# Linear attention on one core: the normaliser's sum over a head's partitions made by accumulating DMA transfers instead of a TensorE product

## The chip, the cores and the metric

The kernel runs on one core of a Trainium2 chip. The metric is the device time of one execution in microseconds; lower is better. Times of a kernel are medians of several runs. A profile is one execution recorded by the hardware profiler; its span runs from the first to the last recorded instruction.

## The reference

Linear attention with 32 heads of 20 dimensions on 2048 rows of 640 columns, in bfloat16:

```python
B, S, D = x.shape                       # 1, 2048, 640
H = 32; Dh = D // H                     # 20
q, k, v = (x @ wqkv) split into heads
phi = lambda t: where(t > 0, t + 1, exp(t)) + 1e-6
pq, pk = phi(q), phi(k)
kv  = einsum("bhsd,bhse->bhde", pk, v)
z   = pk summed over the rows           # one vector of 20 per head
num = einsum("bhqd,bhde->bhqe", pq, kv)
den = einsum("bhqd,bhd->bhq", pq, z) + 1e-6
out = (num / den, heads joined) @ wo
```

The change concerns `den`: for each row and head, the sum over the head's 20 dimensions of pq times z.

## The kernel before

The work is written out by hand as a list of operations for each engine, in program order. A small planner (`Plan.add`, L35) notes what each operation reads and writes and puts in the semaphore waits; each engine then runs its own list strictly in order (`emit`, L76). TensorE (PE) multiplies, ScalarE (ACT) takes exponentials and logarithms and empties PSUM banks, VectorE (DVE) does the rest of the elementwise work, SyncE (SP) issues nearly all transfers, and GpSimd (POOL) makes constants at the start (`pool_const`, L145).

Stages, in the order of TensorE's list:

1. k = x wk for 16 tiles of 128 rows (L292), phi on ScalarE and VectorE (L305, L307, L310).
2. P = xᵀ phi(k) in two halves of 320 columns (`p_step`, L319). The first half runs over all 16 row tiles, then the second. Five PSUM banks (0 to 4) hold the sums; `p_out` (L331, L334) copies them out. VectorE adds phi(k) over the rows meanwhile (`z_steps`, L366, L387).
3. The queries, in 20 tiles (`q_tile`, L345) of 128 columns by 512 rows: five matmuls each, then an exponential (L353) on ScalarE and two VectorE operations (L357, L360). They are strewn into the second stage and go on behind it. Block s (0 to 3) means rows 512 s to 512 s + 511; each block has five tiles c. The columns are permuted so that partition p of a tile belongs to head p // 4: a head has four partitions in each of the five tiles, 20 in all.
4. `kv_group` (L423) makes kv from P and wv, `kv_mask` (L440) keeps the diagonal blocks, `w2_group` (L447, L451) multiplies by wo, and `w2_rows` (L459) carries the six pieces of the product to their rows with SP transfers.
5. The output: 16 tiles of 128 rows, pq times w2 (`out_mm`, L487), evacuated on ScalarE and VectorE (L524, L509, L512) and sent out by SP (L497).

The normaliser runs beside this. `z_finish` (L397, L401) turns the sums over rows into a column vector zc, with five small matmuls and a VectorE copy. `wsum` (L408, L412) adds pq times zc over the five tiles of a block: one ScalarE operation and four on VectorE, the last into `ub` in bfloat16. `den` (L465) is one TensorE product of `ub` with the head mask `hm`, which sums the four partitions of each head and gives all four the sum. `den_act` (L470, L472) takes the logarithm and exp(-x) of it on ScalarE, into `rd`. `normalize` (L479) multiplies the five pq tiles of the block by `rd` on VectorE, in place; the output products read them.

What sets the order is the main part at the end of the function. `next_q(n)` puts in one query tile and then takes n operations from the list `todo`; `work` appends weighted sums ("w") or normalisations ("n") to it, `pop` takes some off. `inverse(s)` puts in `den` and `den_act` of block s. PSUM banks for query tiles, z and `den` come from a rotating list (`take`): banks 5, 6, 7, and bank 4 as well once the second half of P has been copied out.

Of the kernel before, what the change touches and what calls it, by code (L numbers as in the profile page):

```python
# [82 lines left out]
def bass_standalone__linear_attn_block__prompt_kernel(nc, x, wqkv, wo, out):  # L83
# [11 lines left out]
    with contextlib.ExitStack() as ctx:  # L95
        es = ctx.enter_context

        def sb(name, cols, dt=BF16):
            return es(nc.sbuf_tensor(name, [128, cols], dt))
# [25 lines left out]
        ident = sb("ident", 128)  # L125
        lb = [sb(f"lb{j}", BK, F32) for j in range(2)]
        rd = [sb(f"rd{j}", 2 * BK) for j in range(2)]
        DUO = range(9)
        osb = [sb(f"osb{j}", D) for j in range(4)]
        ps = es(nc.psum_tensor("ps", [128, 8 * BK], F32))  # L130
# [3 lines left out]
        def bank(b, n=BK, off=0, parts=128):  # L134
            return ps[0:parts, BK * b + off:BK * b + off + n]
# [80 lines left out]
        def xT_keys(a, b, cs=range(NC_)):  # L216
            keys = []
            for i, (p, q) in enumerate(XCH):
                if p < b and a < q:
                    keys += [("xT", i)] if i >= NPE else sorted(  # L220
                        {("xT", i, 0 if c < 2 else 2) for c in cs})
            return keys
# [113 lines left out]

        nq = [0]

        def q_tile(sbk, c, b, between=None):
            i = nq[0] % 3  # L340
            nq[0] += 1

            def mm(e):
                for d in range(NC_):
                    r = e.matmul(  # L345
                        bank(b), wqp[:, d * D + 128 * c:d * D + 128 * c + 128],
                        xT[:, d * S + BK * sbk:d * S + BK * (sbk + 1)],
                        start=(d == 0), stop=(d == NC_ - 1))
                return r
            P.add("pe", mm, reads=[("wqp", d) for d in range(NC_)]  # L350
                  + xT_keys(BK * sbk, BK * (sbk + 1)), writes=[("bank", b)])
            t = eq[i]
            P.add("act", lambda e: e.activation(t[:, :], bank(b), ACTF.Exp),  # L353
                  reads=[("bank", b), "table"], writes=[("eq", i)])
            if between:
                between()
            P.add("dve", lambda e: e.tensor_scalar(  # L357
                t[:, :], t[:, :], 1.0, 1e-6, ALU.min, ALU.add),
                reads=[("eq", i)], writes=[("eq", i)])
            P.add("dve", lambda e: e.scalar_tensor_tensor(  # L360
                pq[:, c * S + BK * sbk:c * S + BK * (sbk + 1)], bank(b), 0.0, t[:, :],
                ALU.max, ALU.add),
                reads=[("bank", b), ("eq", i)], writes=[("pq", sbk, c)])
# [40 lines left out]
        def wsum(s, c):  # L404
            v = pq[:, c * S + BK * s:c * S + BK * (s + 1)]
            a, z, key = ua[s % 2], zc[:, c:c + 1], ("ua", s % 2)
            if c == 0:
                P.add("act", lambda e: e.activation(a[:, :], v, ACTF.Copy, scale=z),  # L408
                      reads=[("pq", s, c), "zc"], writes=[key])
                return  # L410
            dst, dkey = (ub[s % 2], ("ub", s % 2)) if c == NC_ - 1 else (a, key)
            P.add("dve", lambda e: e.scalar_tensor_tensor(  # L412
                dst[:, :], v, z, a[:, :], ALU.mult, ALU.add),
                reads=[("pq", s, c), "zc", key], writes=[dkey])
# [49 lines left out]
        def den(s, b):  # L464
            P.add("pe", lambda e: e.matmul(bank(b), hm[:, :], ub[s % 2][:, :], start=True, stop=True),  # L465
                  reads=["hm", ("ub", s % 2)], writes=[("bank", b)])

        def den_act(s, b):
            t = lb[s % 2]
            P.add("act", lambda e: e.activation(t[:, :], bank(b), ACTF.Ln, bias=eps[:, 0:1]),  # L470
                  reads=[("bank", b), "eps", "table"], writes=[("lb", s % 2)])
            P.add("act", lambda e: e.activation(  # L472
                rd[s // 2][:, BK * (s % 2):BK * (s % 2 + 1)], t[:, :], ACTF.Exp, scale=-1.0),
                reads=[("lb", s % 2)], writes=[("rd", s)])
# [94 lines left out]
        def take():  # L569
            small.append(small.pop(0))  # L570
            return small[-1]

        def next_q(n=1, between=None):
            q_tile(*qs.pop(0), take(), between)
            for _ in range(n):
                if todo:
                    todo.pop(0)()
# [13 lines left out]
        def pop(n):  # L591
            for _ in range(n):
                todo.pop(0)()
# [12 lines left out]
        p_out(0)  # L606
        next_q()
        next_q()
        for st in range(NT - 2):
            p_step(1, st)  # L610
            if st in (0, 1):
                zst.pop(0)()
            if st == 5:
                z_finish(take())
                work("w0", "w1", "n0")
                pop(3)
            if st in (1, 4, 7, 10, 12):
                next_q({7: 2, 10: 2}.get(st, 0))
            if st == 11:
                inverse(0)  # L620
        assert not zst
        for d in range(NC_):
            p_step(1, NT - 2, (d,))
            p_step(1, NT - 1, (d,))
        p_out(1)
        pop(3)

        def state_groups():
            kv_group(0)
            kv_mask(0)  # L630
        next_q(0, between=state_groups)
        small.insert(0, 4)

        def first_groups():
            w2_group(0, 2)
# [9 lines left out]
        w2_group(5, 0)  # L645
        next_q(1)
        next_q(1)
        inverse(1)
        work("w20", "n1", "w21234")
        for n in (1, 2, 2):  # L650
            next_q(n)
# [51 lines left out]
```

## Time and profile before

| | |
|---|---|
| median of 3 runs | 99.36 us (99.22 to 99.4) |
| the profiled execution | 99.4 us |
| its span | 98.1 us |
| granted TensorE clock | 1.0 |
| instructions | 1667 |
| transfers | 11.73 MB, all on queues of SP and ACT |
| GpSimd's busy time | 3.5 us, all at the start |

A row of a timeline gives the start and the length in microseconds, the engine, the line of the kernel, the operation, its output and inputs, how many instructions were merged, and in brackets how long the engine had been idle before and what it waited for. "PEld" is TensorE's loading of weights, which runs beside the matmuls. Consecutive matmuls overlap, so a row's length is somewhat longer than the time that it adds to the stream; the chain of work that ended last gives the added time.

### The profile page before, as it was taken

What the parts mean: (1) busy time and instruction counts of PE and PEld (TensorE: products, weight loads), DVE (VectorE), ACT (ScalarE), POOL (GpSimd) and SP (SyncE); (2) the same over time, 40 slices, a digit from 0 to 9 for tenths busy, and PEclk for the clock granted to TensorE, in tenths of its full rate; (3) what the DMA queues carried; (4) which work ended last, traced back from release to release, by engine and by line L of the source; (5) the groups of instructions that cost most, each with busy time, mean ns of one, the idle gap of its engine ahead of it and who ended that gap; (6) DMA issues with size and microseconds to landing.
All of it is one profiled execution on the core that took longest, in us unless ns stands there. A gap on an engine that the chain in (4) does not pass through costs nothing.

```text
span 98.1 us, 1667 instructions
## 1 busy us (share of the span) xinstructions
PE 95.0 (97%) x651; PEld 62.4 (64%) x657; DVE 74.0 (75%) x138; ACT 50.3 (51%) x83; POOL 3.5 (4%) x15
## 2 busy tenths in 40 slices
PE   6999999999999999999999999999999999999991
PEld 2667777777777666555566556755447776677771
DVE  0305987888889897999849759999979998819332
ACT  5107454445698201462042476289796749665321
POOL 6800000000000000000000000000000000000000
DMA  2986899989999920000000000006600223322534
GB/s 47 361 193 131 162 169 135 218 272 379 366 362 284 205 63 10 0 0 0 0 7 0 0 0 0 0 0 165 164 15 0 98 102 134 134 70 73 197 134 134
DMA packets 17236, 11.73 MB, mean 120 GB/s; under 512 B 9933, under 2 KB 17229, under 8 KB 17229
## 3 DMA queue, kind: packets, MB, share of 16 engines
q1 hardware_dynamic: 16653, 11.10, 42.9%
q10 hardware_dynamic: 576, 0.53, 1.6%
q8 instruction: 5, 0.08, 0.4%
q14 instruction: 2, 0.02, 0.1%
HBM read 5.90 MB, written 2.62 MB: 87 GB/s over the span
## 4 chain that ended last, share of the span: by engine, by line
PE 90%; DVE 6%; ACT 1%; issue 0%
PE ps L292 23%; PE ps L487 22%; PE ps L345 21%; PE ps L319 17%; DVE za L366 3%; PE ps L280 3%; PE ps L447 2%; PE ps L423 1%; DVE pq L360 1%; ACT eq L353 1%; PE ps L198 1%; PE ps L465 1%; DVE eq L357 1%; DVE pt L334 0%; DVE osb L512 0%
## 5 line engine op out<-in xcount | busy, mean ns | idle before, releaser
L319 PE MATMUL ps<-pk,xn 128*128 128x320 bf16 x160 | 24.0, 299 | 0.0
L345 PE MATMUL ps<-xT,wqp 128*128 128x512 bf16 x95 | 23.1, 379 | 0.3
L292 PE MATMUL ps<-wk,xT 128*128 128x320 bf16 x160 | 22.9, 305 | 0.0
L487 PE MATMUL ps<-w2p,pq 128*128 128x320 bf16 (+3 forms) x170 | 22.3, 291 | 0.1
L353 ACT ACTIVATE eq<-ps 128x512 bf16<-128x512 f32 x20 | 11.9, 597 | 19.2 <-PE ps L345 19.0
L319 PEld LDWEIGHTS ps<-pk,xn 128*128 128x128 bf16 x160 | 15.6, 98 | 7.5
L292 PEld LDWEIGHTS ps<-wk,xT 128*128 128x128 bf16 x160 | 15.9, 100 | 6.5 <-ACT xT L210 0.2
L487 PEld LDWEIGHTS ps<-w2p,pq 128*128 128x128 bf16 x170 | 15.9, 98 | 6.4 <-DVE pq L479 0.2
L305 ACT ACTIVATE ek<-ps 128x640 bf16<-128x640 f32 x16 | 11.2, 704 | 11.8 <-PE ps L292 11.1
L345 PEld LDWEIGHTS ps<-xT,wqp 128*128 128x128 bf16 x100 | 9.7, 97 | 9.2
L360 DVE SCALAR_TENSOR_TENSOR pq<-ps,eq 128x512 bf16<-128x512 f32 x20 | 13.8, 692 | 0.7
L310 DVE SCALAR_TENSOR_TENSOR pk<-ps,ek 128x640 bf16<-128x640 f32 x16 | 13.2, 825 | 0.5
L412 DVE SCALAR_TENSOR_TENSOR ua<-pq,zc,ua 128x512 f32<-128x512 bf16 x12 | 9.0, 749 | 1.1 <-ACT ua L408 0.9
L307 DVE TENSOR_SCALAR ek<-ek 128x640 bf16<-128x640 bf16 x16 | 5.2, 324 | 5.9 <-ACT ek L305 5.9
L479 DVE TENSOR_TENSOR pq<-pq,rd 128x512 bf16<-128x512 bf16 x20 | 7.4, 418 | 2.8 <-ACT rd L472 2.8
L357 DVE TENSOR_SCALAR eq<-eq 128x512 bf16<-128x512 bf16 x20 | 5.8, 289 | 4.1 <-ACT eq L353 3.9
L524 ACT CAST osb<-ps 128x640 bf16<-128x640 f32 x9 | 6.2, 688 | 3.6 <-PE ps L487 3.4
L512 DVE CAST osb<-ps 128x320 bf16<-128x320 f32 (+2 forms) x8 | 3.5, 434 | 3.3 <-PE ps L487 3.1
L366 DVE TENSOR_TENSOR za<-pk 128x1280 f32<-128x1280 bf16 x4 | 5.8, 1483 | 0.0
L509 ACT CAST osb<-ps 128x320 bf16<-128x320 f32 (+1 forms) x8 | 3.1, 404 | 4.7 <-PE ps L487 4.5
L366 DVE TENSOR_TENSOR za<-za 128x1280 f32<-128x1280 f32 x3 | 4.4, 1482 | 0.0
L270 ACT COPY wqp<-wqn 128x640 bf16<-128x640 bf16 x5 | 4.3, 933 | 0.0
(41 smaller groups left out, 43.5 us busy)
## 6 DMA issues: line engine op xcount, KB each, us to landing
out_dram<-osb SPq DMA_DIRECT2D x15, 160.0 KB, 1.8
xn<-in_x_dram SPq DMA_DIRECT2D x2, 800.0 KB, 10.1
wqn<-in_wqkv_dram SPq DMA_DIRECT2D x1, 800.0 KB, 6.4
wv<-in_wqkv_dram SPq DMA_DIRECT2D x1, 800.0 KB, 13.6
wog<-in_wo_dram SPq DMA_DIRECT2D x1, 750.0 KB, 14.2
w2p<-w2g SPq DMA_DIRECT2D x5, 150.0 KB
xn<-in_x_dram SPq DMA_DIRECT2D x1, 640.0 KB, 7.6
wk<-in_wqkv_dram SPq DMA_DIRECT2D x3, 160.0 KB, 3.4
```

Source lines behind the costliest of these rows:

```text
L292: r = e.matmul(bank(b + h, HALF), xT[:, c * S + 128 * st:c * S + 128 * st + 128], wk[:, c * D + HALF * h:c * D + HALF * (h + 1)], start=(c ...
L305: P.add("act", lambda e: e.activation(fold(t[:, :]), two_banks(b), ACTF.Exp), reads=banks + ["table"], writes=[("ek", st % 3)])
L310: P.add("dve", lambda e: e.scalar_tensor_tensor(fold(pk[:, st * D:(st + 1) * D]), two_banks(b), 0.0, fold(t[:, :]), ALU.max, ALU.add), rea ...
L319: r = e.matmul(bank(d, HALF), xn[:, st * D + 128 * d:st * D + 128 * d + 128], pk[:, st * D + HALF * h:st * D + HALF * (h + 1)], start=(st ...
L345: r = e.matmul(bank(b), wqp[:, d * D + 128 * c:d * D + 128 * c + 128], xT[:, d * S + BK * sbk:d * S + BK * (sbk + 1)], start=(d == 0), sto ...
L353: P.add("act", lambda e: e.activation(t[:, :], bank(b), ACTF.Exp), reads=[("bank", b), "table"], writes=[("eq", i)])
L357: P.add("dve", lambda e: e.tensor_scalar(t[:, :], t[:, :], 1.0, 1e-6, ALU.min, ALU.add), reads=[("eq", i)], writes=[("eq", i)])
L360: P.add("dve", lambda e: e.scalar_tensor_tensor(pq[:, c * S + BK * sbk:c * S + BK * (sbk + 1)], bank(b), 0.0, t[:, :], ALU.max, ALU.add), ...
L366: P.add("dve", lambda e: e.tensor_tensor(d_ap, a, b, ALU.add), reads=ra + rb, writes=[dst])
L412: P.add("dve", lambda e: e.scalar_tensor_tensor(dst[:, :], v, z, a[:, :], ALU.mult, ALU.add), reads=[("pq", s, c), "zc", key], writes=[dkey])
L479: P.add("dve", lambda e: e.tensor_tensor(v, v, rd[i][:, BK * o:BK * (o + 1)], ALU.mult), reads=[("rd", sbk), ("pq", sbk, c)], writes=[("pq ...
L487: r = e.matmul(bank(b, hi - lo), pq[:, c * S + 128 * st:c * S + 128 * st + 128], w2p[:, c * D + lo:c * D + hi], start=(c == 0), stop=(c == ...
```

## The change

For blocks 0 and 1 (rows 0 to 1023) the last weighted sum goes into a new float32 tile `uf`, and the sum over a head's four partitions is made by five transfers in SBUF. Part k is the partitions k, k + 4, k + 8 and so on of `uf`, each delivered to the four partitions of its head. SP copies part 0 into `sa` and part 2 into `sc`. GpSimd then issues three accumulating transfers: part 1 is added to `sa`, part 3 to `sc`, and at last `sc` to `sa`. `den_act` reads `sa`. Blocks 2 and 3 are as before.

In the order: z's products and its copy stand directly behind the matmuls of the seventh query tile, ahead of that tile's exponential, and all five weighted sums of block 0 follow there; they stood one row tile of P later and were strewn between the next tiles. The block's logarithm and exponential move from before the tenth query tile's exponential to behind that of the eleventh; those of block 1 stay behind the seventeenth. The sums of block 1 keep their place but for one operation.

```diff
+        uf = [sb(f"uf{j}", BK, F32) for j in range(2)]
+        sa = [sb(f"sa{j}", BK, F32) for j in range(2)]
+        sc = [sb(f"sc{j}", BK, F32) for j in range(2)]
...
-        def q_tile(sbk, c, b, between=None):
+        def q_tile(sbk, c, b, between=None, behind=None):
...
+            if behind:
+                behind()
             t = eq[i]
             P.add("act", lambda e: e.activation(t[:, :], bank(b), ACTF.Exp),
...
-            dst, dkey = (ub[s % 2], ("ub", s % 2)) if c == NC_ - 1 else (a, key)
+            dst, dkey = (a, key) if c < NC_ - 1 else (
+                (uf[s], ("uf", s)) if s < 2 else (ub[s % 2], ("ub", s % 2)))
...
+        def head_sum(s):
+            def part(k):
+                return uf[s][k:128:4, :].unsqueeze(1).broadcast_to([32, 4, BK])
+
+            def move(eng, dst, src, reads, key, **kw):
+                P.add(eng, lambda e: e.dma_start(dst[:, :], src, **kw),
+                      reads=reads + ([key] if kw else []), writes=[key], dma=True)
+            a, c = ("sa", s), ("sc", s)
+            move("sp", sa[s], part(0), [("uf", s)], a)
+            move("sp", sc[s], part(2), [("uf", s)], c)
+            move("pool", sa[s], part(1), [("uf", s)], a, accum_op=ALU.add)
+            move("pool", sc[s], part(3), [("uf", s)], c, accum_op=ALU.add)
+            move("pool", sa[s], sc[s][:, :], [c], a, accum_op=ALU.add)
+
         def den_act(s, b):
             t = lb[s % 2]
-            P.add("act", lambda e: e.activation(t[:, :], bank(b), ACTF.Ln, bias=eps[:, 0:1]),
-                  reads=[("bank", b), "eps", "table"], writes=[("lb", s % 2)])
+            src, key = (sa[s][:, :], ("sa", s)) if b is None else (bank(b), ("bank", b))
+            P.add("act", lambda e: e.activation(t[:, :], src, ACTF.Ln, bias=eps[:, 0:1]),
+                  reads=[key, "eps", "table"], writes=[("lb", s % 2)])
...
+        def first_sum():
+            z_finish(take())
+            work("w0")
+            pop(5)
+            head_sum(0)
+            work("w1")
+
         for st in range(NT - 2):
             p_step(1, st)
             if st in (0, 1):
                 zst.pop(0)()
-            if st == 5:
-                z_finish(take())
-                work("w0", "w1", "n0")
-                pop(3)
-            if st in (1, 4, 7, 10, 12):
-                next_q({7: 2, 10: 2}.get(st, 0))
-            if st == 11:
-                inverse(0)
+            if st in (1, 7, 10, 12):
+                next_q({7: 3, 10: 1}.get(st, 0))
+            if st == 4:
+                next_q(0, behind=first_sum)
...
         p_out(1)
-        pop(3)
+        pop(1)
+        head_sum(1)
...
         next_q(0, between=state_groups)
         small.insert(0, 4)
+        den_act(0, None)
+        work("n0")
...
-        inverse(1)
+        den_act(1, None)
```

More of the change, by code (lines that the diff above doesn't have):

```diff
@@ L571, in take, with next_q @@
             return small[-1]
-        def next_q(n=1, between=None):
-            q_tile(*qs.pop(0), take(), between)
+        def next_q(n=1, between=None, behind=None):
+            q_tile(*qs.pop(0), take(), between, behind)
             for _ in range(n):
```

## The prediction, made before the changed kernel ran

> **What bounds the kernel now.** I read the page first: busy shares, slices, the chain that ended last. Then, for the stretch that the change touches, the merged timeline of all engines from 47 to 74 us, the weight loads, and the waits of SP's queue. The page:
>
> ```profile
> PE 95.0 (97%) x651; PEld 62.4 (64%) x657; DVE 74.0 (75%) x138; ACT 50.3 (51%) x83; POOL 3.5 (4%) x15
> PE   6999999999999999999999999999999999999991
> PE 90%; DVE 6%; ACT 1%; issue 0%
> ```
>
> TensorE is busy in every slice but the ends; between its first and last matmul it hardly waits. So the time is the sum of TensorE's matmuls: a matmul taken away is time gained, and any wait put before a matmul is time lost, at one to one, for nothing behind it has slack to give back. GpSimd works 3.5 us in all. The chain that ended last, in order of time, shows what the two removed products weigh, and a query tile's five matmuls:
>
> ```profile
> 47.73 1.08 PE ps L345 x5
> ...
> 55.85 0.22 PE ps L465
> ...
> 70.50 0.22 PE ps L465
> ```
>
> L465 is the product with the head mask, one for each 512 rows. Each adds 0.22 us to TensorE's stream; for rows 0 to 1023 there are two. **Gain: 2 x 0.22 = 0.44 us**, and no more, whatever the rest does.
>
> **The change part by part.** Times are in the clock of the profiled execution, span 98.1 us, time 99.40 us; the 1.30 us around the span I leave as they are. The median of the runs is 99.36, so the execution lies 0.04 above it.
>
> The rows that I walk along, from the timeline of all engines:
>
> ```profile
> 46.38 1.32 DVE L387 TENSOR_TENSOR zs<-za 128x640 bf16<-128x640 f32 x1
> 47.57 1.24 PE L345 MATMUL ps<-xT,wqp 128*128 128x512 bf16 x5
> 47.93 0.69 DVE L360 SCALAR_TENSOR_TENSOR pq<-ps,eq 128x512 bf16<-128x512 f32 x1
> 49.33 0.27 PE L397 MATMUL ps<-ones,zs 128*128 128x1 bf16 x5
> 49.81 0.69 DVE L360 SCALAR_TENSOR_TENSOR pq<-ps,eq 128x512 bf16<-128x512 f32 x1
> 50.41 0.15 DVE L401 COPY zc<-ps 128x5 f32<-128x5 f32 x1
> 50.60 0.72 ACT L408 ACTIVATE ua<-pq,zc 128x512 f32<-128x512 bf16 x1 [1.16 <-DVE zc L401]
> 51.45 1.54 DVE L412 SCALAR_TENSOR_TENSOR ua<-pq,zc,ua 128x512 f32<-128x512 bf16 x2 [0.88 <-ACT ua L408]
> 52.91 0.29 DVE L357 TENSOR_SCALAR eq<-eq 128x512 bf16<-128x512 bf16 x1
> 53.23 0.69 DVE L360 SCALAR_TENSOR_TENSOR pq<-ps,eq 128x512 bf16<-128x512 f32 x1
> 53.93 1.24 PE L345 MATMUL ps<-xT,wqp 128*128 128x512 bf16 x5
> ```
>
> *z moved up.* The five z products now come right behind the seventh query tile, whose stream ends at 48.65 (1.08 from 47.57), before the next five state matmuls and not behind them. Their operand zs is complete at 46.38 + 1.32 = 47.70, so they don't wait, and they only change places on TensorE: cost 0. Their result is there at 48.65 + 0.27 = 48.92; VectorE, free since 47.93 + 0.69 = 48.62, copies it at 48.95 and not at 50.41.
>
> *Weighted sums moved up.* ScalarE's first scaling began 0.19 behind the copy (50.41 to 50.60) and VectorE's first addition 0.85 behind that (51.45). So in the new order ScalarE starts at 49.14 and VectorE at 50.0. All four additions now run in one go, ahead of the seventh tile's own two operations. Four such additions stand later in the same trace:
>
> ```profile
> 77.52 2.32 DVE L412 SCALAR_TENSOR_TENSOR ua<-pq,zc,ua 128x512 f32<-128x512 bf16 x3
> 79.87 0.75 DVE L412 SCALAR_TENSOR_TENSOR ub<-pq,zc,ua 128x512 bf16<-128x512 bf16 x1
> 80.54 2.32 DVE L412 SCALAR_TENSOR_TENSOR ua<-pq,zc,ua 128x512 f32<-128x512 bf16 x3
> ```
>
> From 77.52 to 80.54 are 3.02 us for four. The fourth starts 2.35 behind the first and takes 0.75: uf of rows 0 to 511 is written at 50.0 + 3.10 = **53.10** (ub was finished at 54.61 + 0.75 = 55.36 before). A bf16 or float32 result makes no difference (0.75 and 0.77 each). The seventh tile's pair follows at 53.02 and ends 0.33 + 0.69 later, at **54.04**, where it ended at 49.81 + 0.69 = 50.50.
>
> *What this delay holds up.* The query tiles go round three PSUM banks and z takes a turn: tile 7 has bank 5, z 6, tile 8 bank 7, tile 9 bank 5 again. Tile 9's first matmul runs at 53.93 and its weights are loaded ahead:
>
> ```profile
> 53.79 0.88 PEld L345 LDWEIGHTS ps<-xT,wqp 128*128 128x128 bf16 x5
> 64.73 0.60 PEld L447 LDWEIGHTS ps<-wog,kvt 120*120 120x120 bf16 x4
> ```
>
> Now it must wait for tile 7's pair, 54.04 and an assumed 0.03 for the signal. If only the matmul waits, TensorE stands 0.14 us; if the weight load waits too, which starts 0.14 ahead of its matmul, 0.28. Below the two ends lies nothing, for VectorE can't be through earlier than its rows allow. I take the middle: **0.21 us lost**. So from tile 9 on, TensorE has lost 0.21 and saved 0.22, and the old clock holds again. Tiles 10 and 11 have banks 6 and 7, free since 49.1 and about 55. VectorE goes on from 53.96, with 0.33 + 0.60 for a pair until the next operation begins (49.81 to 50.41) and 0.75 for an addition: tile 8's pair until 54.9, two additions of the second block until 56.4, tile 9's pair until 57.3, the third addition until 58.1. Tile 10's pair began at 58.49 when its exponential was there (row below), and does so again, after 0.4 of idle time. The state copies L334 stand where they were.
>
> *Rows 512 to 1023.* Their last addition follows the state copies (below), at 60.22, so uf is written at 60.97. VectorE then has 1.5 us less in front of the mask products, which TensorE didn't wait for visibly: 0.
>
> *The sum over DMA.* In place of one product and its wait, five transfers in three levels, each with its semaphore: SP copies parts 0 and 2 into sa and sc (256 KB each; each of 32 partitions goes to four), GpSimd adds part 1 to sa and part 3 to sc, then adds sc to sa. The trace has no GpSimd transfer and no accumulating one. The nearest rows are SP's:
>
> ```profile
> out_dram<-osb SPq DMA_DIRECT2D x15, 160.0 KB, 1.8
> ```
> ```profile
> L497 SPq DMA_DIRECT2D out_dram<-osb x16: 332/332/382, 76.1 to 96.2; - x16
> DMA to landing us min/median/max: 1.6/1.8/3.7
> ```
> ```profile
> L459 SPq DMA_DIRECT2D w2p<-w2g x6: 697/772/932, 64.7 to 69.3; - x6
> ```
>
> A landing is 1.6 to 3.7 us, 1.8 in the middle, for 160 KB. For SP's copies of 256 KB I put 2.0, an estimate a little above that. An accumulating one reads two operands and is built by another engine; I take 2.8, midway between 1.8 and 3.7. Then: 2.0 for sa, 0.35 until sc has landed (one SP issue of 0.33), 2.8 and 2.8 for the two GpSimd levels, 0.3 assumed for three signals: **T = 8.3 us** from uf to the end, estimated. The lowest the rows allow is 3 x 1.6 + 0.35 = 5.2, the highest 3 x 3.7 + 0.35 + 0.3 = 11.8, or 13.3 with an issue of 0.77 before each GpSimd level.
>
> *Who waits for it.* ScalarE's logarithm, now behind the exponential of tile 11 (at 60.98). What is queued behind it on ScalarE: the exponential of tile 12, the copies of the w2 groups, and through these TensorE.
>
> ```profile
> 56.31 0.68 ACT L470 ACTIVATE lb<-ps,eps 128x512 f32<-128x512 f32 x1
> 57.02 0.63 ACT L472 ACTIVATE rd<-lb 128x512 bf16<-128x512 f32 x1
> 58.49 0.29 DVE L357 TENSOR_SCALAR eq<-eq 128x512 bf16<-128x512 bf16 x1 [0.97 <-ACT eq L353]
> 59.43 0.88 DVE L334 CAST pt<-ps 128x320 bf16<-128x320 f32 x2
> 60.22 1.53 DVE L412 SCALAR_TENSOR_TENSOR ua<-pq,zc,ua 128x512 f32<-128x512 bf16 x2
> 60.78 1.59 PE L423 MATMUL ps<-pt,wv 128*128 128x120 bf16 x30
> 60.98 0.60 ACT L353 ACTIVATE eq<-ps 128x512 bf16<-128x512 f32 x1 [0.65 <-PE ps L345]
> 63.50 0.60 ACT L353 ACTIVATE eq<-ps 128x512 bf16<-128x512 f32 x1 [1.92 <-PE ps L345]
> 63.99 0.69 ACT L451 CAST w2g<-ps 120x640 bf16<-120x640 f32 x1
> 71.03 0.68 ACT L470 ACTIVATE lb<-ps,eps 128x512 f32<-128x512 f32 x1
> 73.79 0.43 PE L487 MATMUL ps<-w2p,pq 128*128 128x320 bf16 x2
> ```
>
> ScalarE is idle for 1.92 us between 61.58 and 63.50. Logarithm and exponential take 0.71 + 0.63 = 1.34 together (0.04 more if an SBUF operand costs what L408's 0.72 shows): they fit there at no cost if the sum has landed by 63.50 - 1.34 = **62.16**. Beyond that the copy of w2 group 0 (63.99 to 64.68) comes late, and its banks are wanted by the load at 64.73: no slack left. From 53.10 this gives the chain **9.06 us**. With T = 8.3 it lands at 61.4, 0.76 early: cost 0. If that cover is gone, each us of lateness costs one.
>
> *The second sum* starts at 60.97 and is wanted at 71.03, where the logarithm stood before: 10.06 us, so 0 too; and TensorE needs rows 512 to 1023 only four output tiles behind 73.79. Its GpSimd transfers wait behind the first sum's last issue (about 58.5), long past. On SP its two issues stand before the first w2 transfer; SP waits there anyway:
>
> ```profile
> SPq L459 <- ACT w2g L451: 38.5, 4, 36.9
> ```
>
> with 36.9 us of it ahead of 64.70. The transfers themselves run beside those of w2 from 64.7 on. These are nearly all landed before 72, and the first user is at 73.79, so about 1.8 us of sharing cost nothing:
>
> ```profile
> 70.00:71.00 1.00, 1.00 (x7) 0.41 (x6) 0.97 (x3) 0.52 (x2) 0.00 (x0) 1.00 0.62 127
> 72.00:73.00 1.00, 1.00 (x7) 0.47 (x5) 0.48 (x2) 1.00 (x3) 0.00 (x0) 1.00 0.02 8
> ```
>
> (The last two columns are the transfers' share and GB/s.)
>
> *Sum:* 99.40 - 0.44 + 0.21 = **99.17 us**; 98.96 if the stall at tile 9 doesn't come, 99.24 if it comes whole. That is 0.2% below the execution and sits on the edge of what a measurement here can tell from no change, which is about 0.2%.
>
> **The rivals.**
>
> *B, the chain is late (slower).* The place is ScalarE's logarithm before tile 12. It decides from T = 9.06 on. For it: GpSimd's transfers are unseen, and three landings in series have little room; against it: the median landing is half the slowest. With landings of 3.7 on both GpSimd levels and an issue of 0.33 ahead of each, T = 2.0 + 0.35 + 2 x (3.7 + 0.33) + 0.3 = 10.7, 1.65 late: 99.17 + 1.65 = 100.8. With 3.7 and no issue of its own, 10.05: 100.2. I take 100.4, between.
>
> *C, VectorE and GpSimd hold each other up (slower).* VectorE has two L357 operations between the SP landing (about 55.3) and the state copies, for tiles 9 and 10. If each had to stand still for a GpSimd issue as long as the longest issue row, 0.93, VectorE would come 1.86 late. It has about 0.4 idle before tile 10's pair, and the state product at 60.78 has 0.5 over the copies (59.43 + 0.88 = 60.31): 0.96 is left, 99.17 + 0.96 = 100.1. No row shows GpSimd at work beside VectorE, so nothing bears on it but how full VectorE is. The Trainium skill's page "SBUF — State Buffer", section "Who interferes with whom", says that VectorE in its two-port modes and GpSimd lock each other out of a shared port pair for a whole instruction, and that a transfer issued by GpSimd then starves for descriptors. No trace here shows it yet.
>
> *D, the change doesn't give what it takes away.* TensorE loses the products and gets the time back as waits: 0.28 at tile 9 and, as VectorE runs without a gap from 50 to 59, some 0.2 before the state product. 99.40 - 0.44 + 0.48 = 99.44. For it: VectorE's pair of tile 7 is 3.5 us later; against: the 0.5 of slack just named.
>
> **How the numbers follow.** The forecast (in time, a stall of 0 to 0.28 at tile 9, 98.95 to 99.3) has 0.54: 0.35 of it under 99.16, 0.18 within, 0.01 above. B has 0.30: 0.28 slower, 0.02 within. C 0.09: 0.08 slower, 0.01 within. D 0.07: 0.05 within, 0.02 slower. Faster by over 0.2%: 0.35; within: 0.26; slower: 0.39. The likeliest single case is the forecast, with its own range 98.95 to 99.3; for 8 in 10 the range reaches into B: 98.95 to 100.9. It leaves out the chain of 11.8 us and more (all levels at their slowest at once), which would give 101.9, and 103.4 at 13.3 us.
>
> **What would show it.** In the new profile: two L465 rows fewer on TensorE, 0.44 us. Before tile 9, a weight load that waited for VectorE's pq, 0.1 to 0.3. No ScalarE wait for a transfer at the logarithm, or one that ends before 62.2 in a clock where tile 12's matmuls stand at 62.22; a wait that ends later, with TensorE idle before the w2 groups by the same amount, is B. An L357 longer than 0.29, or begun late beside a GpSimd issue, is C. I am wrong in size if TensorE idles somewhere that I put at 0, and wrong in kind if the time around the span moves.

## The result, and the profile after

| | before | changed |
|---|---|---|
| median | 99.38 us (6 runs) | 104.7 us (6 runs) |
| the profiled execution | 99.40 us | 104.47 us |
| its span | 98.1 us | 103.2 us |

The changed kernel takes 1.0521 times as long, with a 95% interval of 1.0495 to 1.0548: slower by about 5.2%, where 0.2% faster was forecast. Some executions ran slower at a lower granted clock (two of the changed kernel's six, 106.3 us at 0.968) and are left out of the ratios, though the medians count them; one experiment was run a second time for that.

The page of the changed kernel, the lines that answer to those shown of before (busy shares, slices, shares of the chain that ended last):

```profile
PE 95.4 (92%) x655; PEld 61.8 (60%) x655; DVE 74.4 (72%) x138; ACT 50.3 (49%) x83; POOL 8.9 (9%) x21
PE   6999999999999999999989999259988997999992
PE 61%; DVE 17%; DMA 13%; ACT 4%; issue 2%; SPq 1%; ACTq 0%; POOLq 0%
```

TensorE is busy for the same 95 us, but there is a hole in the middle (the slices with 2 and 5, 64.5 to 69.7 us), and transfers now have 13% of the chain, where none were listed. The waits of the changed kernel (engine, output and line, what it waited for: us in all, times, longest) name what ended each hole:

```profile
ACT lb L491 <- DMA sa<-sc: 6.0, 2, 4.1
...
PE ps L453 <- ACT w2g L457: 3.1, 1, 3.1
...
PE ps L508 <- DMA w2p<-w2g: 0.8, 1, 0.8
...
PE ps L471 <- DVE ub L418: 0.6, 1, 0.6
...
PE ps L348 <- DVE pq L365: 0.4, 1, 0.4
```

TensorE waits in four places that had no wait before. The largest is the second group of w2 products (L453), which waits for ScalarE's copies; and ScalarE itself waited 4.1 us at one logarithm (L491) for the last accumulating transfer. The timeline of all engines along that path, in the changed kernel (start, length; the POOL rows of L479 are GpSimd's three issues for the first sum, SPq L465 are the issues of the w2 rows):

```profile
47.22 1.24 PE L348 MATMUL ps<-xT,wqp 128*128 128x512 bf16 x5
48.60 0.17 DVE L406 COPY zc<-ps 128x5 f32<-128x5 f32 x1 [0.32 <-PE ps L402]
48.80 0.72 ACT L413 ACTIVATE ua<-pq,zc 128x512 f32<-128x512 bf16 x1 [2.83 <-DVE zc L406]
50.05 2.33 DVE L418 SCALAR_TENSOR_TENSOR ua<-pq,zc,ua 128x512 f32<-128x512 bf16 x3 [1.28 <-ACT eq L358]
52.41 0.75 DVE L418 SCALAR_TENSOR_TENSOR uf<-pq,zc,ua 128x512 f32<-128x512 bf16 x1
...
54.15 1.25 PE L348 MATMUL ps<-xT,wqp 128*128 128x512 bf16 x5 [0.41 <-DVE pq L365]
56.24 1.00 POOL L479 DMA_DIRECT2D sa<-uf  x1 [51.60 <-DVE ua L418]
56.92 1.24 POOL L479 DMA_DIRECT2D sc<-uf  x1
61.48 0.84 POOL L479 DMA_DIRECT2D sa<-sc  x1 [3.32 <-DMA sc<-uf]
65.69 0.72 ACT L491 ACTIVATE lb<-sa,eps 128x512 f32<-128x512 f32 x1 [4.09 <-DMA sa<-sc]
68.16 6.19 SPq L465 DMA_DIRECT2D w2p<-w2g  x6
68.19 0.75 PE L453 MATMUL ps<-wog,kvt 120*120 120x320 bf16 x4 [3.08 <-ACT w2g L457]
76.34 0.72 ACT L491 ACTIVATE lb<-sa,eps 128x512 f32<-128x512 f32 x1 [1.90 <-DMA sa<-sc]
```

Read from the top: uf is written at 52.41 + 0.75 = 53.16, the first sum is complete when the logarithm starts, at 65.69. **T = 12.5 us**; 8.3 was estimated, and up to 9.06 was to cost nothing. ScalarE stands at the logarithm, behind it the w2 copies, behind these TensorE. (GpSimd's first wait is put down to VectorE's ua, but VectorE was through with that at 52.41; what came last is the landing of sa.) The w2 rows go out from 68.16, where they went out from 64.70, and the second sum's logarithm runs at 76.34.

How much each place took shows when the same matmuls start in both traces. Before, beside the rows that the prediction quotes:

```profile
64.92 0.71 PE L447 MATMUL ps<-wog,kvt 120*120 120x320 bf16 x4
...
86.47 9.70 PE L487 MATMUL ps<-w2p,pq 128*128 128x320 bf16 x80
```

And in the changed kernel:

```profile
77.80 7.63 PE L508 MATMUL ps<-w2p,pq 128*128 128x320 bf16 x55 [0.75 <-DMA w2p<-w2g]
...
91.53 9.70 PE L508 MATMUL ps<-w2p,pq 128*128 128x320 bf16 x80
```

| matmuls | before | changed | behind | lost or gained since the row above |
|---|---|---|---|---|
| query tile 7 | 47.57 | 47.22 | -0.35 | the start of this execution |
| query tile 9 | 53.93 | 54.15 | 0.22 | 0.57 lost to VectorE |
| second w2 products | 64.92 | 68.19 | 3.27 | 0.22 gained (one product), 3.27 lost to the first sum |
| first output products | 73.79 | 77.80 | 4.01 | 0.22 gained, 0.96 lost, w2p late |
| last 80 output products | 86.47 | 91.53 | 5.06 | 1.05 lost, block 2's weighted sum and what followed it late |

5.06 is the difference of the spans (5.1). So three things cost: the order, 0.57; the first sum, 3.3; the second, some 2.0 in two places. With the 0.44 saved and the early start of 0.35 that is 99.40 - 0.44 + 0.57 + 3.27 + 2.01 - 0.35 = 104.46, against 104.47 profiled. The second sum was to cost nothing. Two of its transfers, in the chain of work that ended last in the changed kernel (issue, time to its landing):

```profile
61.58 4.28 DMA sc<-uf
...
69.93 6.39 DMA sa<-sc
```

### The profile page after: what moved, and what is told of

The parts are those of the page before. It is cut to its first block, busy times and chain, and to the rows that moved or that the text cites. A ratio compares the mean times of both kernels' runs of the same rounds, so it can differ in the third digit from the quotient of the medians.

```text
span 103.2 us, 1686 instructions
## 1 busy us (share of the span) xinstructions
PE 95.4 (92%) x655; PEld 61.8 (60%) x655; DVE 74.4 (72%) x138; ACT 50.3 (49%) x83; POOL 8.9 (9%) x21
## 4 chain that ended last, share of the span: by engine, by line
PE 61%; DVE 17%; DMA 13%; ACT 4%; issue 2%; SPq 1%; ACTq 0%; POOLq 0%
PE ps L295 21%; PE ps L322 15%; PE ps L508 11%; PE ps L348 10%; DMA sc<-uf 7%; DVE ua L418 6%; DMA sa<-sc 6%; DVE pq L500 3%; DVE pq L365 3%; PE ps L283 3%; ACT eq L358 2%; DVE uf L418 1%; ACT ua L413 1%; PE ps L201 1%; DVE eq L362 1%
## 5 line engine op out<-in xcount | busy, mean ns | idle before, releaser
L348 PE MATMUL ps<-xT,wqp 128*128 128x512 bf16 x100 | 24.0, 379 | 0.4 <-DVE pq L365 0.4
L358 ACT ACTIVATE eq<-ps 128x512 bf16<-128x512 f32 x20 | 11.8, 594 | 16.9 <-PE ps L348 16.8
L308 ACT ACTIVATE ek<-ps 128x640 bf16<-128x640 f32 x16 | 11.2, 704 | 11.4 <-PE ps L295 10.7
L479 POOL DMA_DIRECT2D sa<-uf x2 | 1.9, 938 | 53.2 <-DVE ua L418 51.6
L453 PE MATMUL ps<-wog,kvt 120*120 120x320 bf16 x12 | 2.3, 303 | 3.1 <-ACT w2g L457 3.1
```

Source lines behind the costliest of these rows:

```text
L308: P.add("act", lambda e: e.activation(fold(t[:, :]), two_banks(b), ACTF.Exp), reads=banks + ["table"], writes=[("ek", st % 3)])
L348: r = e.matmul(bank(b), wqp[:, d * D + 128 * c:d * D + 128 * c + 128], xT[:, d * S + BK * sbk:d * S + BK * (sbk + 1)], start=(d == 0), sto ...
```

## The experiments

The theory after the result: accumulating transfers of GpSimd are slow, and three levels of them don't fit into the time that the order leaves. The rivals: VectorE and GpSimd hold each other up; the order alone costs it; the transfers cost because other transfers run beside them. Line numbers below are those of each kernel. Ratios stand against the kernel before, run on the same chip.

**1. The order without the sum.** The transfers are gone, and the logarithm reads uf.

```diff
-            src, key = (sa[s][:, :], ("sa", s)) if b is None else (bank(b), ("bank", b))
+            src, key = (uf[s][:, :], ("uf", s)) if b is None else (bank(b), ("bank", b))
...
-            head_sum(0)
...
-        head_sum(1)
```

> The changed kernel without its ten transfers: the logarithm of blocks 0 and 1 reads uf itself, so the sum over a head's four partitions is left out there. Theory (the chain is the loss): only the new order and the two missing products remain, 99.4 - 0.44 + 0.57 for the stall seen before the ninth tile = 99.5, between 99.2 and 99.7, and TensorE idle under 0.7 us between 50 and 85 us. Rival (the new order of VectorE's and ScalarE's work costs the time): still above 102.

Measured: 99.45 us, 1.0013 (0.9985 to 1.004). Of the changed kernel's four new waits of TensorE only the last one shown is left in this kernel's waits, a query tile's for VectorE, with the same 0.4.

So some 5 us come with the transfers. But two products are gone and the time hasn't fallen: the new order eats about 0.44 by itself.

**2. The order with the two products back.**

```diff
-        den_act(0, None)
+        inverse(0)
...
-        den_act(1, None)
+        inverse(1)
```

> The changed kernel's order with the two products back on TensorE, each right ahead of its logarithm; no transfers. Theory: 0.44 above the kernel that leaves the sum out, so 99.8 to 100.1. Rival (the order costs the time): above 102.5.

Measured: 99.9 us, 1.0048 (1.0021 to 1.0074), 0.45 more than without the products by the medians, 0.35 by the ratios, whose intervals just touch. That agrees with the predicted worth of two products, 0.44, without being a sharp measurement of it; the order costs 0.5.

**3. The order with another bank for z.** As experiment 1, but z's PSUM bank is taken ahead of tile 7's, so that tile 9 reuses z's bank and not tile 7's.

```diff
+                zb.append(take())
                 next_q(0, behind=first_sum)
...
-            z_finish(take())
+            z_finish(zb[0])
```

> The kernel with the order alone (no transfers, the sum over a head's partitions left out), and z takes its PSUM bank ahead of the seventh tile, so that the ninth tile's bank is z's and not the seventh tile's. Theory (0.5 us of the order's cost is the ninth tile's wait for its bank): 98.85 to 99.05, and no wait of TensorE for VectorE there. Rival (VectorE is late everywhere, the wait moves to another tile): 99.3 to 99.5.

Measured: 98.86 us, 0.9951 (0.9927 to 0.9976). TensorE no longer waits for VectorE; tile 9 in this timeline, without a bracket:

```profile
54.02 1.24 PE L348 MATMUL ps<-xT,wqp 128*128 128x512 bf16 x5
```

What the order cost was one bank. With it freed, the products' 0.44 shows, and this is the most that a sum at no cost could give in this order.

**4. The transfers by themselves.** The kernel before, and behind its last output the chain of five transfers on a scratch tile, twice at rest, twice beside 50 VectorE operations of L357's form, twice beside 22 of L412's; then single transfers. Its time says nothing of the change, only its trace is read.

```diff
+        for r in range(2):
+            mark(chain(f"q{r}x"))
+        for r in range(2):
+            k = chain(f"s{r}x")
+            busy_scalar(50)
+            mark(k)
...
+        single("gpfull", "pool", uf[:, :])
+        single("gppart", "pool", part(1))
+        single("gafull", "pool", uf[:, :], acc=True)
+        single("gapart", "pool", part(1), acc=True)
+        single("gahalf", "pool", wkt[0][:, :], BF16, acc=True)
```

> The kernel of before, and behind its last output the disputed transfers alone, all other engines at rest: twice the chain of five, twice the chain beside 50 VectorE operations of L357's form, twice beside 22 of L412's form, then single transfers, three of each in a row: SP plain, GpSimd plain, GpSimd accumulating, in float32 and bfloat16. Theory (an accumulating GpSimd transfer takes 3.5 to 4.5 us by itself): chain 11 to 12.5 us in all three settings. Rival (VectorE locks GpSimd out): 9 us or less at rest, over 11 beside L357's form. Rival (accumulating costs nothing, GpSimd's issue does): plain and accumulating ones of GpSimd within 0.3 us of each other, and both over 1 us above SP's.

The DMA issues of this kernel (output and input, queue, count, size, median us from issue to landing); "csc" is filled by two transfers in flight with "csa", "gp" are plain transfers of GpSimd, "ga" accumulating ones, "part" has each of 32 partitions go to four:

```profile
csa<-mf SPq DMA_DIRECT2D x6, 256.0 KB, 2.4
...
csa<-mf POOLq DMA_DIRECT2D x6, 256.0 KB, 3.3
csc<-mf POOLq DMA_DIRECT2D x6, 256.0 KB, 4.3
csa<-csc POOLq DMA_DIRECT2D x6, 256.0 KB, 3.3
...
gppart<-mf POOLq DMA_DIRECT2D x3, 256.0 KB, 2.3
gapart<-mf POOLq DMA_DIRECT2D x3, 256.0 KB, 3.3
```

GpSimd's queue is not slow: a plain transfer lands in 2.3 us, as SP's. Accumulating costs 1.0 us more, and with two accumulating ones in flight the second takes 4.3. Copied partition by partition, without the spreading to four, both take the same (2.3 and 3.3). The first chain at rest, and one beside VectorE, in the timeline of this kernel:

```profile
99.90 0.64 SPq L682 DMA_DIRECT2D csa<-mf  x1
...
102.95 1.01 POOL L682 DMA_DIRECT2D csa<-mf  x1 [98.31 <-DMA csa<-mf]
...
108.22 0.84 POOL L682 DMA_DIRECT2D csa<-csc  x1 [3.34 <-DMA csc<-mf]
...
123.13 16.79 DVE L699 TENSOR_SCALAR eq<-eq 128x512 bf16<-128x512 bf16 x51
123.22 0.52 SPq L682 DMA_DIRECT2D csa<-mf  x1
...
131.70 0.84 POOL L682 DMA_DIRECT2D csa<-csc  x1 [3.18 <-DMA csc<-mf]
```

At rest the chain takes 108.22 + 3.3 - 99.90 = 11.6 us, and 11.3 the second time; beside L357's form 131.70 + 3.3 - 123.22 = 11.8, and 11.3; beside L412's 11.3 and 11.6. With nothing else at work on the core it is already 2.2 to 2.5 longer than the 9.06 that the order leaves. VectorE isn't the cause. (The kernel ran once, and each chain's end is taken from the median landing of its last transfer, 3.3.)

**5. The same five transfers, all plain and all on SP.** Nothing is added up; dependences and sizes stay.

```diff
-            move("pool", sa[s], part(1), [("uf", s)], a, accum_op=ALU.add)
-            move("pool", sc[s], part(3), [("uf", s)], c, accum_op=ALU.add)
-            move("pool", sa[s], sc[s][:, :], [c], a, accum_op=ALU.add)
+            move("sp", sa[s], part(1), [("uf", s)], a)
+            move("sp", sc[s], part(3), [("uf", s)], c)
+            move("sp", sa[s], sc[s][:, :], [c], a)
```

> All five transfers issued by SP as plain copies, same sizes, same three levels and same waits; the additions are left out. Theory (GpSimd's accumulating transfers are slow): three landings of 2.4 to 3.0 us, the chain takes 8 to 9 us from uf and just fits into the 9.06 us: 99.4 to 100.0. Rival (any chain of three transfers in SBUF takes this long, whoever issues it): 12 us, and over 103.5.

Measured: 101.38 us, 1.0197 (1.0152 to 1.0241); 99.4 to 100.0 had been expected. The timeline of this kernel:

```profile
53.56 0.66 SPq L479 DMA_DIRECT2D sa<-uf  x1
...
61.86 0.71 ACT L491 ACTIVATE lb<-sa,eps 128x512 f32<-128x512 f32 x1
...
66.79 0.49 SPq L479 DMA_DIRECT2D sa<-sc  x1
67.33 5.79 SPq L465 DMA_DIRECT2D w2p<-w2g  x6
...
75.73 2.47 PE L508 MATMUL ps<-w2p,pq 128*128 128x320 bf16 x17 [1.61 <-DVE pq L365]
```

The logarithm starts 61.86 - 53.56 = 8.3 us behind the first issue, and it has no wait in brackets: the first sum was there by then. So T is at most 8.3, the value of the estimate (7.9 if its last transfer, issued at 59.17, lands after the median 2.3), and block 0 is free. The loss lies elsewhere. SP runs its queue in order, and the second sum's last transfer stood at its head until 66.79, so the w2 rows went out from 67.33 and not from 64.70, and the first output products waited 1.6 us. (The row names a pq of VectorE's. In experiment 6, with the same order, that one was written at 75.36, after the same products had begun at 74.77: it isn't what they need. That leaves the w2 rows; this is argued from the two traces.)

**6. All ten transfers, and nobody waits for them.** As experiment 1, with the transfers put back.

```diff
-            src, key = (sa[s][:, :], ("sa", s)) if b is None else (bank(b), ("bank", b))
+            src, key = (uf[s][:, :], ("uf", s)) if b is None else (bank(b), ("bank", b))
...
+        out_keys += [("sa", 0), ("sa", 1)]
```

> The changed kernel with all ten transfers, but nothing on ScalarE waits for them: the logarithm of blocks 0 and 1 reads uf itself, so the sum over a head's four partitions is made and not used. Theory (the wait at ScalarE is the loss): as the kernel with the order alone, 99.3 to 99.7. Rival (the transfers share engines and queues with the w2 rows, and that costs): 100.3 or more, with TensorE waiting for w2p before the first output product.

Measured: 100.65 us, 1.0119 (1.0085 to 1.0152), against 1.0013 without the transfers: 1.1 us for traffic alone, give or take 0.4. The theory had 99.3 to 99.7, its rival 100.3 or more. The waits of this kernel, in its timeline the last issue of the second sum, and in the chain of work that ended last the last of the w2 rows (issue, time to its landing):

```profile
PE ps L508 <- DMA w2p<-w2g: 0.7, 1, 0.7
```
```profile
73.15 0.85 POOL L479 DMA_DIRECT2D sa<-sc  x1 [5.75 <-DMA sc<-uf]
```
```profile
69.61 5.07 DMA w2p<-w2g
```

The second sum and the w2 rows (65 to 74 us) slow each other down: GpSimd sat idle for 5.75 us until sc had landed, where the chain at rest has 3.34, SP's six issues of w2 rows took 6.06 us, where they took 5.29 before, and the last row landed at 74.68, so late that the output products waited until 74.77. The last packets ahead of that stand in 73.8 to 74.1 of a table by stretches of 0.3 us, so this landing counts 0.6 to 0.9 us behind its packets. The other 4 us of the loss come only when something waits for the sum.

**7. The sum by transfers for block 0 alone**, block 1 with its product.

```diff
-                (uf[s], ("uf", s)) if s < 2 else (ub[s % 2], ("ub", s % 2)))
+                (uf[s], ("uf", s)) if s < 1 else (ub[s % 2], ("ub", s % 2)))
...
-        head_sum(1)
...
-        den_act(1, None)
+        inverse(1)
```

> The changed kernel with only block 0 summed by transfers; block 1 by its product on TensorE, right ahead of its logarithm. Theory: the wait before the twelfth tile stays (3.3 us), and of the later waits (w2p 0.96, block 2's sum 0.8, 0.28) those that come from the second sum go: if the w2p wait is a consequence of the first wait, which pushes the w2 copies together, 103.5 to 104.2; if it comes from the second sum's traffic, 102.7 to 103.2.

The first run of this kernel carries no verdict; what follows is its repetition:

> The kernel with only block 0 summed by transfers, once more, since its first comparison rested on one undisturbed run (102.34): 102.2 to 102.6, and a wait of 2.4 to 3.1 us before the third w2 group.

Measured: 102.49 us, 1.0316 (1.0271 to 1.0361). The waits of the repetition:

```profile
ACT lb L491 <- DMA sa<-sc: 3.4, 1, 3.4
...
PE ps L453 <- ACT w2g L457: 2.4, 1, 2.4
```

Against experiment 1 with one product's 0.22 on top, the first sum costs (1.0316 - 1.0013) x 99.4 - 0.22 = 2.8 us; the second then (1.0521 - 1.0316) x 99.4 + 0.22 = 2.3; both give or take 0.5. No wait for w2p is left here. The first logarithm waits less than in the changed kernel (3.4 against 4.1): block 0's last transfer is issued at 62.33 and the logarithm stands at 65.59, 3.3 us as at rest, where it took 4.2 beside block 1's transfers.

**8. Copies on SP, additions on GpSimd.** The changed kernel with experiment 3's bank: four plain copies, and three tensor additions computed on GpSimd in place of the accumulating transfers.

```diff
+            add(t0, t1, k0, k1)
+            add(t2, t3, k2, k3)
+            add(t0, t2, k0, k2)
```

> The changed kernel with the bank as in the run beside it, and with the sum made by four plain SP copies into four tiles and three GpSimd additions of 128x512 float32, in place of accumulating transfers; nothing is left out. Theory (the loss is the length of the chain): copies landed 2.4 to 4.2 us behind uf, three additions of some 1.0 to 1.3 us each, 6.5 to 8 us in all, less than the 9.06 us that are there: 98.9 to 99.2, under the kernel of before. Rival (GpSimd's additions and VectorE's two-operand ones slow each other): additions above 2 us or L418 above 0.8, and 99.5 or more.

Measured: 101.13 us, 1.0193 (1.0154 to 1.0231); 98.9 to 99.2 had been expected. The timeline of this kernel:

```profile
57.70 1.70 POOL L485 TENSOR_TENSOR sc<-sc,sg 128x512 f32<-128x512 f32 x1
58.19 1.36 DVE L364 TENSOR_SCALAR eq<-eq 128x512 bf16<-128x512 bf16 x1
...
60.83 0.71 ACT L499 ACTIVATE lb<-sa,eps 128x512 f32<-128x512 f32 x1
```

The sum is in time (60.83), but a VectorE operation that lasts 0.29 elsewhere takes 1.36 beside GpSimd's addition, and TensorE waits for VectorE. Here VectorE and GpSimd do hold each other up, as rival C has it, but with GpSimd's computing and not with its transfers. In the changed kernel the group of that operation has its old length:

```profile
L362 DVE TENSOR_SCALAR eq<-eq 128x512 bf16<-128x512 bf16 x20 | 5.8, 290 | 7.3 <-ACT eq L358 7.0
```

**9. The last level on VectorE.** The changed kernel with experiment 3's bank: two copies and two accumulating transfers, then one VectorE addition of sc to sa, for both blocks.

```diff
-            move("pool", sa[s], sc[s][:, :], [c], a, accum_op=ALU.add)
+
+        def last_add(s):
+            P.add("dve", lambda e: e.tensor_tensor(sa[s][:, :], sa[s][:, :], sc[s][:, :], ALU.add),
+                  reads=[("sa", s), ("sc", s)], writes=[("sa", s)])
```

> The changed kernel with z's bank taken first, and with the last of the three levels made by VectorE (sa + sc, 128x512 float32) instead of a transfer; nothing is left out. Theory (the length of the chain decides): 2.4 + 0.6 + 0.7 + 4.3 + 0.7 = 8.7 us, in time, so ScalarE's logarithm of block 0 begins by 62.2 and TensorE doesn't wait before the w2 groups; what stays is up to 0.7 of waiting for w2p beside block 1's transfers: 98.9 to 99.7. If the logarithm is still late by over 1 us, or the time over 100.5, the chain isn't what it was taken for.

Measured: 100.91 us, 1.0141 (1.0108 to 1.0174); 98.9 to 99.7 had been expected. The timeline of this kernel:

```profile
62.10 0.72 ACT L494 ACTIVATE lb<-sa,eps 128x512 f32<-128x512 f32 x1 [0.95 <-DVE sa L488]
...
72.72 0.72 ACT L494 ACTIVATE lb<-sa,eps 128x512 f32<-128x512 f32 x1 [1.87 <-DVE sa L488]
74.80 5.46 PE L511 MATMUL ps<-w2p,pq 128*128 128x320 bf16 x39 [1.34 <-DMA w2p<-w2g]
```

The hole before the w2 products is gone. Block 0's logarithm stands at 62.10. This execution runs 0.43 ahead of the one before (tile 12's matmuls at 61.79, there 62.22), so the deadline of 62.16 is 61.73 here: the logarithm is 0.4 late, and the second group of w2 products comes 1.73 behind the first (62.87 to 64.60), where it came 1.62 behind before. Of 0.4 us of lateness TensorE lost 0.1. What is left is the second block: its logarithm at 72.72, and 1.34 us for w2p.

**10. Block 0's sum consumed late.** The changed kernel with experiment 3's bank: all five transfers for block 0 with their logarithm put far back, behind tile 15, block 1 with its product, and block 2's first sums moved up into the free place. The edit also moves block 2's scaling from ScalarE to VectorE, one operation of 0.48 us.

```diff
-        den_act(0, None)
-        work("n0")
+        work("w2012")
...
+        next_q(0)
+        den_act(0, None)
         w2_group(5, 0)
-        next_q(1)
-        next_q(1)
-        den_act(1, None)
-        work("w20", "n1", "w21234")
+        work("n0")
```

> Block 0 by all five transfers, block 1 by its product, z's bank taken first; block 0's logarithm and normalisation stand some 8 us later (behind the fifteenth tile), with block 2's first sums in their old place; nothing is left out. Theory: the chain of 12 us is covered, nobody waits for it, 0.22 gained: 98.9 to 99.3, no wait of ScalarE for a transfer. Rival (transfers and the rest disturb each other even when nobody waits): over 99.6.

Measured: 100.29 us, 1.0103 (1.0073 to 1.0134); 98.9 to 99.3 had been expected. Nobody but GpSimd waits for a transfer of the sum now. But VectorE's work has moved with the logarithm, and two query tiles wait for banks that it empties; the waits of this kernel:

```profile
PE ps L348 <- DVE pq L365: 1.0, 2, 0.6
```

A chain of 11 us can be hidden. This order, with the later normalisation and the added scaling on VectorE, costs 1.2 us against experiment 3 with one product more (98.86 + 0.22); no run tells the two apart.

**11. Block 0 by experiment 9, block 1 with its product.** Everything is computed.

```diff
-                (uf[s], ("uf", s)) if s < 2 else (ub[s % 2], ("ub", s % 2)))
+                (uf[s], ("uf", s)) if s < 1 else (ub[s % 2], ("ub", s % 2)))
...
-        head_sum(1)
...
-        last_add(1)
-        den_act(1, None)
+        inverse(1)
```

> Block 0 by two SP copies, two accumulating transfers and a last addition on VectorE (in time in the run with both blocks: its logarithm began at 62.10), block 1 by its product, z's bank taken first; nothing is left out. Theory (block 1's transfers, which meet the w2 rows, cost what was left): no wait for w2p or for a transfer, one product fewer, 98.86 + 0.22 = 99.1, and up to 0.3 more for the wait at the w2 groups: 99.0 to 99.4, equal to the kernel of before or a little under it. Rival (block 0's transfers cost something even when in time): over 99.7.

Measured: 99.26 us, 0.9982 (0.9962 to 1.0003), and TensorE waits nowhere for a sum. One product less is worth 0.22, and the ratio agrees with that but can't be told from no change. It is the fastest of the versions here that compute everything with transfers in the sum.

**12. The exponential ahead of the scaling.** In experiment 1 VectorE's first addition starts 0.4 later than walked; the row names ScalarE's exponential, issued right behind the scaling. Here it stands ahead.

```diff
-            if behind:
-                behind()
             t = eq[i]
...
+            if behind:
+                behind()
```

> The order alone (no transfers, the sum over a head's partitions left out), with the seventh tile's exponential on ScalarE ahead of the first scaling of block 0 and not behind it. In all runs with the new order VectorE's first addition began 0.53 us behind the end of that scaling, at the end of the exponential behind it; in the kernel of before, with nothing behind the scaling, 0.13. Theory (ScalarE's signal comes late when the next instruction follows at once): VectorE begins 0.13 behind the scaling's end, some 0.2 us earlier than with the order alone, the ninth tile waits some 0.2 less, 99.2 to 99.35. Rival (the scaling from SBUF needs this time by itself): 0.5 again and 99.5 or more.

Measured: 99.62 us, 1.0019 (0.999 to 1.0048); 99.2 to 99.35 had been expected. The timeline of this kernel:

```profile
49.19 0.71 ACT L413 ACTIVATE ua<-pq,zc 128x512 f32<-128x512 bf16 x1
...
50.43 2.33 DVE L418 SCALAR_TENSOR_TENSOR ua<-pq,zc,ua 128x512 f32<-128x512 bf16 x3 [1.46 <-ACT ua L413]
```

The gap from the end of the scaling (49.90) to the addition is 0.53 again, as in the changed kernel (49.52 to 50.05), and was 0.13 before (51.32 to 51.45). Nothing follows on ScalarE now, so the theory that the next instruction held up the signal falls. The cause stays open.

## Why the prediction was wrong, by its own steps

- **Two products, 0.44 saved: right.** Experiments 1 and 2 differ by 0.35 to 0.45; experiment 3 shows the gain itself (1 - 0.9951, 0.49 us, 0.24 to 0.73).
- **z moved up, 0: right.** The copy of z stands 0.3 behind the z products, and these didn't wait.
- **Weighted sums moved up:** the four additions took 53.16 - 50.05 = 3.11 (3.10 walked), but began 0.4 later than walked (50.05, where 50.0 - 0.35 = 49.65 in this execution's clock). Why is open (experiment 12).
- **Tile 9's bank, 0.21 lost: the mechanism right, the size too small.** 0.57 in the trace, 0.6 between experiments 1 and 3. The load and its matmul start together at 54.15, so the load's lead of 0.14 is slack and the lower of the two bounds, 0.14, was the right one; the rest is VectorE's lateness, 54.15 against 54.07 - 0.35 = 53.72, 0.43. With that alone the forecast would have been 99.5, no gain.
- **The failed step: "The sum over DMA", T = 8.3.** Term by term: SP's copy 2.4 (2.0 assumed), 0.64 until GpSimd starts (0.1 of the signals), 0.68 until its second issue (0.35), the second accumulating transfer 4.3 (2.8), the signal 0.28 (0.1), the last one 4.2 (2.8; 3.3 at rest). The chain at rest is 11.3 to 11.6. The step took the landing of an accumulating transfer from plain SP stores, and set it between their median and their slowest; the rows held no accumulating transfer. Its upper bound, 11.8, is close to the chain at rest, but by luck: it has 3.7 at every level, where 2.4, 4.3 and 3.3 were measured, and the waits ahead of GpSimd's issues make up the rest. The range left that end out as "all levels at their slowest at once"; but the two GpSimd levels weren't slow by chance, they are of one kind and slow together. Even that end, priced at 101.9, stays below 104.7: the second sum's cost is missing in it.
- **The deadline, 9.06, and one to one beyond it: right but for some 0.25 us of slack.** In time (experiment 5) block 0 is free; 0.4 late (experiment 9) it costs 0.1; in the changed kernel the logarithm is 65.69 - 62.18 = 3.5 late (62.18 is the deadline in its clock, where tile 12's matmuls stand at 62.24), and TensorE loses 3.3. The step counted from the weight load at 64.73; in the changed kernel load and matmul start together (68.19), so the load's lead of 0.19 before its matmul at 64.92 is slack, as at tile 9.
- **The second sum and the sharing with w2, 0: wrong.** It costs 2.0 by the trace and 2.3 by experiment 7, of 5.3 in all. 10.06 us were thought ample for 8.3. It took 76.34 - 60.99 = 15.35, and two of its transfers were far longer than at rest: SP's copy of part 2 took 4.28 beside the first sum's last transfer, issued at 61.48 (2.5 in experiment 4, and in experiment 9, where that transfer is left out), and the last accumulating transfer took 6.39 beside the w2 rows (3.3 at rest). And the w2 rows came late for the output. Traffic that nobody waits for costs 1.1 (experiment 6). The slack before the first output product was read as 1.8 us from the packets' end. In a table by stretches of 0.3 us, the last packets of the kernel before stand in 72.2 to 72.5; if a landing counts 0.6 to 0.9 behind them as in experiment 6, the slack was 0.4 to 1.0.
- **SP's queue, 0: right as ordered.** SP's two issues wait for nothing late. Once the second sum's later levels stand there too, the w2 rows wait behind them, and the output products 1.6 us for the rows (experiment 5, argued there).
- **Rival B had the mechanism and the place**, but was priced to T = 10.7 and had nothing behind the w2 products: 100.4 for 104.7.
- **Rival C fell for transfers and holds for additions on GpSimd.** The Trainium skill's page "SBUF — State Buffer", section "Who interferes with whom", has transfers issued by GpSimd starve beside VectorE's two-port operations. In experiment 4 the chain took 11.8 and 11.3 us beside 50 operations of L357's form and 11.6 and 11.3 at rest: 0.5 at most, in one of two. The lock that the same section describes between the two engines' instructions shows in experiment 8, 1.36 us for 0.29.
- **Rival D is what the order alone does**: 99.45 measured in experiment 1, 99.44 priced. It came from one place (the bank), not from two, so that the two numbers agree is in part luck.

## What to carry to other kernels

A sum over partitions by accumulating transfers is a chain of latencies: count its levels, price each by a measured transfer of that very kind, and compare the chain with the time between the last producer and the first engine that stands in order behind it. Where no row shows the kind, don't treat levels of one kind as independent: here both accumulating levels were slower than the value taken for them, together. Count the transfers that it delays as well, even if nobody waits for its own, and look at which buffer a moved step takes from a rotating list: one bank was worth more here than both products.

## What the runs showed of the hardware that was not expected

- An accumulating float32 transfer of 256 KB inside SBUF lands after 3.3 us, a plain one after 2.3, from the same queue; with two accumulating ones in flight the second took 4.3. The Trainium skill's page "DMA: Bandwidth & Descriptors", section "Anatomy of one DMA — SWDGE (gpsimd) path", fits 2.0 us plus the bytes over 436,000 per us, which makes an estimate of 2.6 for either: the plain one is faster here, the accumulating one slower.
- GpSimd's next issue started 0.28 us behind the landing that it waited for in the single transfers of experiment 4, and 0.5 to 0.6 behind the landing of SP's copy in its two chains at rest (102.95 against 99.90 + 2.44, 114.59 against 111.72 + 2.35); no run here shows what makes the difference.
- VectorE's start behind ScalarE was 0.53 us in one place and 0.13 in another, for the same pair of operations; no run here shows why.
